# A fused adaLN attention block: projection steps get a pair of row maxima, and steps 105 to 120 do three maxima instead of four

## The chip, the cores and the metric

The kernel runs on one core of a Trainium2 chip. The metric is the device time of one execution in microseconds (us). A profiled execution gives, beside its time, a trace of every instruction on the engines: TensorE (PE, with its weight loads PEld), VectorE (DVE), ScalarE (ACT), GpSimd (POOL), SyncE (SP) and the DMA queues.

## The reference, cut to what matters

For one sequence of 2048 tokens with 448 features the block computes adaptive layer norm, 16-head attention with heads of 28 features, its output projection, a second adaptive layer norm and a GELU MLP.

```python
q, k, v = qkv[0], qkv[1], qkv[2]              # 16 heads of 28
scores = jnp.einsum("bhqd,bhkd->bhqk", q, k) * scale
p = _softmax(scores, axis=-1)                 # needs max over all 2048 keys of each row
o = jnp.einsum("bhqk,bhkd->bhqd", p, v)
x = x + ga * (o @ wo)                         # output projection, gated residual
h = _layernorm(x) * (1 + cb) + sb
x = x + gb * mlp(h)                           # LayerNorm, gelu(h @ w1 + b1) @ w2 + b2
```

## The kernel before

**Three stages.** A first stage builds q, k and v for all heads. The attention stage then runs 16 units of 16 steps, 256 steps in all. A unit is four heads (a group `g`, heads `j` = 0 to 3) and 512 queries (`qt`). Step `kt` of a unit takes 128 keys. The last stage is the MLP.

**One attention step.** PE forms the transposed scores of the four heads in two halves (L1305, 12 matmuls, 28 or 29 rows each). Each half fills a PSUM tile of two banks. ACT takes the exponential of each half into SBUF (L1318). PE then multiplies the exponentials *of the step before* with v into `o` (`av`, L1263). The 29th row of the scores carries minus the row maximum.

**Row maxima.** That maximum must be known before a unit starts, so the kernel computes scores of later units a second time with queries on partitions (`max_mm`, L476, one 28-row matmul of 512 keys) and reduces them on DVE over the free axis (L481). One unit needs 64 of these. They are spread over the steps of the units ahead of it. There are several ways to place them:

- `emit_single`: one matmul into one bank (`m1` or `m2`), one DVE reduction (L481).
- `open_pair` and `close_pair`: the difference of two key blocks (tile `d0h`) gives a matmul and a ReLU on ACT (L643). The step after next adds the second matmul and one DVE operation (L650), which together give two maxima.
- `emit_pair`: two matmuls of two heads next to each other into one PSUM tile of two banks, and one DVE reduction over both (L686). Where no two fitting maxima are left it falls back to two single ones in the same tile.

**Ring and no ring.** `RING` is the step from which a third two-bank tile `s2` is opened in place of the banks of `m2` (`third_tile`). From there a step does one `emit_single` into `m1` and one `emit_pair` into whichever of `s0` and `s2` the scores do not use. That is three maxima. `extra` can add a fourth when the maxima still to do, counted with the three per step to come, would miss a unit's start. Before `RING` a step does up to four singles (even steps) or three, or a closing and two singles (odd steps).

**Projection steps.** The last group's units project as they go. `is_wo` is true for steps 8 to 11 of units 12 to 15, which are steps 200 to 203, 216 to 219, 232 to 235 and 248 to 251. In each, after `av`, one token block is projected (`t_wo`, L396, a chain of 9 or 12 matmuls over 128 rows, called "the chain" below). ACT copies the result (L1052), POOL adds it to the residual. While maxima are left such a step is no ring step: `m2` takes the banks of `s2` back, scores go to `s1` and `s0`, and the step does `WO_MAX` = 3 singles. When no maxima are left, `three` becomes true and the scores rotate over `s1`, `s0` and `s2`.

The order of all instructions on each engine is the order in which this code is written out; no scheduler moves anything. A PSUM tile is written again only after its readers are done.

Of the kernel before, what the change touches and what calls it, by code (L numbers as in the profile page):

```python
# [31 lines left out]
NTT = S // 128  # L32
P1RATE = 4
LAST_MAX = NKT - 4
RING = 121
PAIR_AT = (2, 2, 0, 2)
PAIR_ROWS = {(0, 2): 2, (0, 3): 3, (1, 0): 2, (1, 1): 2, (1, 2): 3}
WO_MAX = 3
# [6 lines left out]
def tile_adaln_block(ctx: ExitStack, tc: tile.TileContext, x, wqkv, wo, w1, b1, w2, b2, c, w_mod, out):  # L45
# [29 lines left out]
    def nm(t):  # L75
        uid[0] += 1
        return f"{t}_{uid[0]}"
# [20 lines left out]
    def ps_two(key):  # L98
        return ps_pools[key][1].tile([128, 2, 512], F32, tag=key, name=nm(key), bufs=1)
# [403 lines left out]
    def load_hi(kind, g, b):  # L503
        loaded[(kind, g, b)] = clock[0] + (5 if clock[0] >= RING else 3)
        tg = ("kh" if kind else "qh") + str(b)
        t = sb.tile([128, 512], F32R, tag=tg, name=nm(tg), bufs=1)
        (kh_sb if kind else qh_sb)[(g, b)] = t
        sp.dma_start(f(t), f(dscr[kind][0][g])[:, b * 512 : (b + 1) * 512])
        if kind and b in (PAIR_AT[g], PAIR_AT[g] + 1) and all((g, PAIR_AT[g] + c) in kh_sb for c in range(2)):
            at(clock[0] + 4, lambda: make_kd(g))  # L510
# [81 lines left out]
    def there(kind, g, b):  # L592
        return (g, b) in (qh_sb, kh_sb)[kind] and loaded.get((kind, g, b), 0) <= clock[0]

    def ready_max():
        return [m for m in mxq if there(1, m[0], m[2]) and there(0, *m[:2])][: 24 if clock[0] >= RING else 64]

# [5 lines left out]
    def make_kd(g):  # L603
        if clock[0] >= RING:
            return
        if g and any(m[0] == kd["g"] for m in pairable()):
            at(clock[0] + 2, lambda: make_kd(g))
            return
        c0 = PAIR_AT[g]
        kd.update(g=g, t=slot("d0h", [128, 1, 512]), **{"from": clock[0] + 1})  # L610
        pool.tensor_tensor(out=kd["t"][:, 0, :], in0=f(kh_sb[(g, c0 + 1)]), in1=f(kh_sb[(g, c0)]), op=ALU.subtract)
# [4 lines left out]
    def pairable():  # L616
        return [
            m for m in mxq
            if m[2] == PAIR_AT[m[0]] and m[4] > 1 and other(m) in mxq and m[3] < PAIR_ROWS.get(m[:2], 4)
        ]  # L620

    def kept_back():
        kept = set()
        n = 0
        for m in pairable()[: (RING - clock[0]) // 2] if clock[0] < RING else ():
            n += 1
            if n <= (NKT * (m[0] * NB + m[1] - 1) + LAST_MAX - clock[0]) // 2 - 1:
                kept.update((m, other(m)))
        return kept
# [26 lines left out]
    def emit_single(half, ps):  # L656
# [9 lines left out]
        m = (alone or same[-2:] or fits or near)[0]  # L666
        if clock[0] < RING:
            kept = kept_back()
# [7 lines left out]
    def emit_pair(half, t):  # L676
        near = ready_max()
        for a, m in enumerate(near):
            n = m[:4] + (m[4] + 1,)
            if m[4] == 2 * half and n in near:  # L680
                mxq.remove(m)
                mxq.remove(n)
                g, qt, cch, i, j = m
                for jj in range(2):
                    max_mm(g, qt, i, j + jj, kh_sb[(g, cch)], lambda: t[:, jj])
                dve.tensor_reduce(out=mxp[(g, qt)][:, i, j : j + 2, cch], in_=t, op=ALU.max, axis=AX.X)  # L686
                count(g, qt, [cch, cch])
                return
        for jj in range(2):
            emit_single(half, lambda: t[:, jj])  # L690
# [38 lines left out]
    def finish_max(g, qt):  # L729
        if px_open and px_open[0][0][:2] == (g, qt):  # L730
            close_pair()
        while left[(g, qt)] > 0:
            emit_max(1)
# [47 lines left out]
    def load_q(u):  # L781
        g, qt = divmod(u, NB)
        qst[u] = load_parts(f"b{u % 2}", 0, g, slice(qt * 512, (qt + 1) * 512))
# [452 lines left out]
    three = False  # L1236


    def is_wo(s_):
        return s_ // NKT >= NU - NB and 8 <= s_ % NKT < 12  # L1240

    def extra(s_):
        if is_wo(s_):
            return False
        most = 0
        need = 0
        for v in range(s_ // NKT + 1, NU):
            need += left.get(divmod(v, NB), 64)
            rest = range(s_, NKT * (v - 1) + LAST_MAX)
            n_wo = sum(is_wo(x) for x in rest)  # L1250
            n_plain = len(rest) - n_wo
            if n_plain > 0:
                most = max(most, (need - 3 * n_plain - WO_MAX * n_wo) / n_plain)
        due[0] += min(most, 1)
        if due[0] < 1:
            return False
        due[0] -= 1
        return True

    def av(u, kt, p, o):  # L1260
        g = u // NB
        for j in range(4):
            pe.matmul(  # L1263
                o[32 * j : 32 * j + 32, :], v_sb[kt // 4][:, kt % 4, 4 * g + j, :], p[j // 2][:, j % 2, :],
                start=(kt == 0), stop=(kt == NKT - 1),
            )
# [4 lines left out]
    for u in range(NU):  # L1271
        g, qt = divmod(u, NB)
        for kt in range(NKT):
            step = u * NKT + kt
            if kt == 2 and u + 1 < NU and u + 1 not in qst:
                load_q(u + 1)
            clock[0] = step
            if kt == LAST_MAX and u + 1 < NU:
                finish_max(*divmod(u + 1, NB))
            tick_late()  # L1280
            if not (three or mxq or late):
                three = True
                s_ring[:] = ["s1", turns[step % 2], turns[1 - step % 2]]
            now[0] = turns[step % 2]
            was, ring = ring, step >= RING and (three or not is_wo(step))
            first = step % 2 if ring else 0
            pt = {hf: slot(tags[step % len(tags)], [128, 2, 512], F32) for hf, tags in zip((first, 1 - first), ptags)}
            if ring != was:
                third_tile(ring)
            more = ring and not three and extra(step)  # L1290
            late_one, after = after, more
            n_max = 0 if ring else WO_MAX if is_wo(step) else 4 - step % 2
            n0 = 1 if step % 4 == 3 and not is_wo(step) else 2
            closing = bool(px_open) and step % 2 == 1

            ks, qs = kst[(g, kt // 4)], qst[u]
            kc = slice((kt % 4) * 128, (kt % 4 + 1) * 128)
            for n, hf in enumerate((first, 1 - first)):
                s2 = ps_s2() if three else ps_two(now[0] if ring and n else ("s1", "s0")[n])
                for term, (kp, qp) in enumerate(((0, 0), (1, 0), (0, 1))):  # L1300
                    if ring and n == 1 and term == 2 and mxq:
                        emit_pair(first, ps_two(turns[1 - step % 2]))
                    for jj in range(2):
                        rows_ = slice(64 * hf + 32 * jj, 64 * hf + 32 * jj + DH + (term == 0))
                        pe.matmul(s2[:, jj, :], ks[rows_, kp, kc], qs[rows_, qp, :], start=(term == 0), stop=(term == 2))  # L1305
                    if closing:
                        if (n, term) == (0, 0):
                            close_pair()
                    elif n == 0 and term < n0 <= n_max:
                        emit_single(1, ps_mx)  # L1310
                    if n == 1 and term == 2:
                        for _ in range(2 if closing else n_max - n0):
                            emit_single(0, ps_mx)
                    if ring and (n, term) == ((1, 0) if late_one else (0, 0)) and not three:
                        emit_single(1 - first, ps_mx)
                    if n == 1 and term == 2 and more:
                        emit_single(first, ps_mx)
                act.activation(pt[hf], s2, AF.Exp, scale=SCALE)  # L1318
            if step == 0:
                v_task(NB - 1, 3, ps_mx())  # L1320
            if pend is not None:
                pu, pkt, pp, po = pend
                av(pu, pkt, pp, po)
                if pkt == NKT - 1:
                    end_unit(pu, po)
            if step % 2 and step + 2 < RING:
                open_pair()
            if kt == 0:
                o = ps_o()
            pend = (u, kt, pt, o)  # L1330
            if qt == NB - 1 and kt % 4 == 3 and g + 1 < NG:
                load_k(g + 1, kt // 4 if g else kt // 4 ^ 2)
            for fn in sched.pop(step, ()):
                fn()
# [115 lines left out]
```

## Time and profile before

| what | value |
|---|---|
| median of three runs | 1113.06 us (1112.14, 1113.06, 1167.62) |
| profiled execution, its time | 1112.02 us |
| span of its instructions | 1110.0 us |
| PE busy | 1098.9 us (99%) |
| DVE busy | 807.2 us (73%) |
| ACT busy | 693.0 us (62%) |
| POOL busy | 213.9 us (19%) |
| granted PE clock | 1.00 |

The span is the time from the first to the last instruction in the profile; the execution's own time is 2.0 us longer. Busy shares are means over three stages with different limits, so they say little of one step. One of the three runs is 5% above the other two.

### The profile page before, as it was taken

Reading aid. Unit: us, or ns where it says so; the run is one execution under the profiler, and the core shown is the slowest. Engines: PE = TensorE matmul, PEld = TensorE weight load, DVE = VectorE, ACT = ScalarE, POOL = GpSimd, SP = SyncE. Lnnn points to the kernel's source line nnn. Section 1 sums busy time; section 2 is a strip of 40 time slices with the busy share of each in tenths; the row PEclk is TensorE's granted clock in tenths of the full one; section 3 lists DMA queues with packets and bytes.
Section 4 is the critical chain, followed back from the end, with each engine's and each line's share of the span. In section 5 each row is a group of like instructions: output and inputs, shape, how many; then the busy total and the mean of one; then the engine's idle time right before and its main releaser. Section 6 shows DMA issues by size and latency. Waiting matters only on the chain.

```text
span 1110.0 us, 20703 instructions
## 1 busy us (share of the span) xinstructions
PE 1098.9 (99%) x8319; PEld 665.7 (60%) x8319; DVE 807.2 (73%) x1394; ACT 693.0 (62%) x877; POOL 213.9 (19%) x214
## 2 busy tenths in 40 slices
PE   8999999999999999999999999999999999999998
PEld 6756775444444444444444454545568888888887
DVE  6968788999999999988888867584558844434322
ACT  4565657888888888888888878677752311111210
POOL 1533333110000000000000020217215414023000
PEclk9999999999999999999999999999999999999999
DMA  9563263120231211221211402112222100000000
GB/s 309 204 195 102 88 204 112 51 68 30 79 94 42 81 34 52 73 83 48 88 31 59 130 24 88 58 30 78 72 82 67 32 34 1 2 32 1 34 1 34
DMA packets 49341, 81.19 MB, mean 73 GB/s; under 512 B 12311, under 2 KB 18702, under 8 KB 49234
## 3 DMA queue, kind: packets, MB, share of 16 engines
q1 hardware_dynamic: 48762, 79.14, 22.6%
q8 instruction: 65, 1.06, 0.4%
q10 hardware_dynamic: 148, 0.46, 0.1%
q0 software_dynamic: 336, 0.28, 0.1%
q14 instruction: 30, 0.25, 0.1%
HBM read 55.04 MB, written 26.48 MB: 73 GB/s over the span
## 4 chain that ended last, share of the span: by engine, by line
PE 95%; DVE 2%; ACT 1%; issue 1%; DMA 1%; SPq 0%; POOL 0%; DVEq 0%; ACTq 0%; POOLq 0%
PE s L1305 23%; PE o L1263 23%; PE m L396 16%; PE pa L396 9%; PE m L476 8%; PE s L1385 3%; PE s L1386 3%; PE s L1384 3%; PE s L476 2%; PE t L1385 1%; PE t L1386 1%; PE t L1384 1%; PE o L277 1%; DMA slot_c<-in_w_mod_dram 1%; DVE mxp L481 1%
## 5 line engine op out<-in xcount | busy, mean ns | idle before, releaser
L481 DVE TENSOR_REDUCE mxp<-m 128x1 f32<-128x512 f32 x563 | 364.6, 685 | 75.5 <-PE m L476 57.7
L1305 PE MATMUL s<-slot_b,slot_a 28*128 28x512 f32 (+1 forms) x3072 | 358.1, 424 | 0.3 <-ACT slot_c0h L1318 0.3
L1305 PEld LDWEIGHTS s<-slot_b,slot_a 28*128 28x128 f32 (+1 forms) x3072 | 210.9, 183 | 172.3 <-ACT slot_c L1318 93.9
L476 PE MATMUL m<-kh,qh 28*128 28x512 f32 x615 | 229.3, 468 | 0.6 <-DVE mxp L481 0.3
L1318 ACT ACTIVATE slot_c<-s 128x1024 f32<-128x1024 f32 x170 | 174.7, 1028 | 53.2 <-PE s L1305 52.3
L1263 PE MATMUL o<-slot_c,v 128*32 128x512 f32 x680 | 178.8, 605 | 0.0
L1361 ACT ACTIVATE full<-m,b_col 128x512 f32<-128x512 f32 x56 | 38.5, 688 | 191.9 <-PE m L396 179.7
L1263 PE MATMUL o<-slot_c1h,v 128*32 128x512 f32 x512 | 134.7, 605 | 0.9 <-ACT slot_c1h L1318 0.9
L1263 PE MATMUL o<-slot_c0h,v 128*32 128x512 f32 x512 | 134.7, 605 | 0.0
L1318 ACT ACTIVATE slot_c0h<-s 128x1024 f32<-128x1024 f32 x128 | 131.5, 1028 | 2.4 <-PE m L396 2.4
L1318 ACT ACTIVATE slot_c1h<-s 128x1024 f32<-128x1024 f32 x128 | 130.7, 1021 | 0.0
L686 DVE TENSOR_REDUCE mxp<-s 128x2 f32<-128x1024 f32 x103 | 126.2, 1226 | 5.1
L1364 DVE CAST hi<-full 128x512 fp32r<-128x512 f32 x56 | 25.5, 456 | 134.5 <-ACT full L1361 134.5
L1318 ACT ACTIVATE slot_d<-s 128x1024 f32<-128x1024 f32 x86 | 88.4, 1028 | 26.2 <-PE s L1305 25.5
L476 PEld LDWEIGHTS m<-kh,qh 28*128 28x128 f32 x615 | 92.0, 182 | 16.6 <-DVE mxp L481 13.1
L1019 POOL TENSOR_TENSOR osb<-osb,osb 128x512 f32<-128x512 f32 x16 | 21.0, 1314 | 363.6 <-DMA osb<-drec 220.9
L1263 PE MATMUL o<-slot_d,v 128*32 128x512 f32 x344 | 90.5, 605 | 0.4 <-ACT osb L1227 0.4
L396 PE MATMUL m<-y,slot_a 128*128 128x512 f32 x160 | 60.6, 395 | 0.0
L481 DVE TENSOR_REDUCE mxp<-ma 128x1 f32<-128x512 f32 x61 | 39.5, 681 | 13.3 <-PE m L476 8.9
L650 DVE CUSTOM_DVE_ANT_0 slot_d0i<-m,slot_d0i 128x512 f32<-128x512 f32 x54 | 37.3, 691 | 15.1 <-PE m L476 9.4
L1365 DVE TENSOR_TENSOR lo<-full,hi 128x512 fp32r<-128x512 f32 x56 | 43.8, 782 | 5.9 <-DVE hi L1364 0.9
L1263 PEld LDWEIGHTS o<-slot_c,v 128*32 128x32 f32 x680 | 24.5, 108 | 39.1 <-issue 36.6
(341 smaller groups left out, 1843.9 us busy)
## 6 DMA issues: line engine op xcount, KB each, us to landing
slot_b<-d SPq DMA_DIRECT2D x32, 256.0 KB
slot_a<-d SPq DMA_DIRECT2D x32, 256.0 KB
d<-lo SPq DMA_DIRECT2D x28, 256.0 KB
d<-hi SPq DMA_DIRECT2D x16, 256.0 KB
osb<-drec SPq DMA_DIRECT2D x15, 256.0 KB
out_dram<-xn SPq DMA_DIRECT2D x16, 224.0 KB
raw<-in_B_w_dram SPq DMA_DIRECT2D x14, 224.0 KB
qh<-d SPq DMA_DIRECT2D x12, 256.0 KB
```

What stands on the lines that cost most here:

```text
L396: pe.matmul(p, a, b, start=(i == 0), stop=(i == len(terms) - 1))
L476: pe.matmul(m, qh_sb[(g, qt)][js, i * 128 : (i + 1) * 128], k[js, :], start=True, stop=True)
L481: dve.tensor_reduce(out=mxp[(g, qt)][:, i, j, cch : cch + 1], in_=m, op=ALU.max, axis=AX.X)
L686: dve.tensor_reduce(out=mxp[(g, qt)][:, i, j : j + 2, cch], in_=t, op=ALU.max, axis=AX.X)
L1263: pe.matmul(o[32 * j : 32 * j + 32, :], v_sb[kt // 4][:, kt % 4, 4 * g + j, :], p[j // 2][:, j % 2, :], start=(kt == 0), stop=(kt == NKT - 1),
L1305: pe.matmul(s2[:, jj, :], ks[rows_, kp, kc], qs[rows_, qp, :], start=(term == 0), stop=(term == 2))
L1318: act.activation(pt[hf], s2, AF.Exp, scale=SCALE)
L1361: act.activation(gf, p, AF.Gelu_apprx_tanh, bias=b1_col[:, i : i + 1])
L1365: dve.tensor_tensor(out=glo, in0=gf, in1=f(ghi), op=ALU.subtract)
L1384: pe.matmul(pp, ghi[:, ts], w_hi, start=(m == 0), stop=False)
L1385: pe.matmul(pp, ghi[:, ts], w_lo, start=False, stop=False)
L1386: pe.matmul(pp, glo[:, ts], w_hi, start=False, stop=(m == NFT - 1))
```

## The change

`RING` goes from 121 to 105. In projection steps that still have maxima to do, a pair goes into tile `s1` after `av`, ahead of the chain. `extra` counts five maxima per projection step instead of three.

```diff
-RING = 121
+RING = 105
@@ extra
-                most = max(most, (need - 3 * n_plain - WO_MAX * n_wo) / n_plain)
+                most = max(most, (need - 3 * n_plain - (WO_MAX + 2) * n_wo) / n_plain)
@@ the attention loop
                 av(pu, pkt, pp, po)
+                if is_wo(step) and not three:
+                    emit_pair(step % 2, ps_two("s1"))
                 if pkt == NKT - 1:
                     end_unit(pu, po)
```

The total of maxima stays the same. Steps 105 to 120 did 64 of them and now do 48; steps 83 to 104 did 87 and now do 86. Steps 200 to 203 and 216 to 219 did 12 each and now do 20 each; steps 232 to 235 did 9 (three in each of 232, 233, 234) and now do 10 (five in 232 and 233). `extra` adds no fourth maximum in either kernel.

**Place 1, PE at step 105.** In these rows `s0`, `s1`, `s2`, `m1`, `m2` are PSUM tiles; L1305 are scores, L476 maxima, L1263 is `av`. Before:

```order
L1305 MATMUL s1_1472_5942<-slot_b0_1259_5100,slot_a2_976_3992 128x512 x2
L476 MATMUL m2_1473_5945<-kh0_1168_4740,qh1_970_3963 128x512
L1305 MATMUL s1_1472_5942<-slot_b0_1259_5100,slot_a2_976_3992 128x512 x4
L1305 MATMUL s0_1474_5953<-slot_b0_1259_5100,slot_a2_976_3992 128x512 x6
L476 MATMUL m1_1475_5960<-kh3_1234_4998,qh1_970_3963 128x512
L476 MATMUL m2_1476_5963<-kh3_1234_4998,qh1_970_3963 128x512
L1263 MATMUL o_1394_5642<-slot_c1_1462_5906,v2_231 32x512 x2
L1263 MATMUL o_1394_5642<-slot_c0h_1463_5907,v2_231 32x512 x2
L476 MATMUL m2_1477_5971<-slot_d0h_1269_5143,qh1_970_3963 128x512
```

And now:

```order
L1305 MATMUL s1_1468_5938<-slot_b0_1259_5100,slot_a2_976_3992 128x512 x2
L476 MATMUL m1_1469_5941<-kh2_1233_4996,qh1_970_3963 128x512
L1305 MATMUL s1_1468_5938<-slot_b0_1259_5100,slot_a2_976_3992 128x512 x4
L1305 MATMUL s2_1470_5949<-slot_b0_1259_5100,slot_a2_976_3992 128x512 x4
L476 MATMUL s0_1471_5954<-kh2_1233_4996,qh1_970_3963 128x512 x2
L1305 MATMUL s2_1470_5949<-slot_b0_1259_5100,slot_a2_976_3992 128x512 x2
L1263 MATMUL o_1392_5638<-slot_c1_1458_5898,v2_231 32x512 x2
L1263 MATMUL o_1392_5638<-slot_c0h_1459_5899,v2_231 32x512 x2
```

Two of the four maxima matmuls have become a pair in the free tile `s0`, the one with `d0h` is gone, and the second half of the scores is in `s2`.

**Place 2, PE at step 201, a projection step, from the second half of the scores to the start of the chain.** Here L396 is the chain. Before:

```order
L1305 MATMUL s0_2174_9075<-slot_b0_2005_8305,slot_a2_2071_8616 128x512 x6
L476 MATMUL m1_2175_9082<-kh3_1834_7509,qh2_1698_6888 128x512
L1263 MATMUL o_2109_8783<-slot_c1_2160_9011,v2_231 32x512 x2
L1263 MATMUL o_2109_8783<-slot_c0h_2161_9012,v2_231 32x512 x2
L396 MATMUL m2_2176_9090<-slot_e0_486_2027,slot_a2h_2087_8685 128x448
```

And now:

```order
L1305 MATMUL s0_2132_8981<-slot_b0_1963_8213,slot_a2_2029_8524 128x512 x6
L476 MATMUL m1_2133_8988<-kh2_1798_7456,qh2_1682_6917 128x512
L1263 MATMUL o_2066_8689<-slot_c1_2116_8910,v2_231 32x512 x2
L1263 MATMUL o_2066_8689<-slot_c0h_2117_8911,v2_231 32x512 x2
L476 MATMUL s1_2134_8996<-kh0_1717_7085,qh2_1682_6917 128x512 x2
L396 MATMUL m2_2135_9000<-slot_e0_486_2027,slot_a2h_2044_8591 128x448
```

Two maxima matmuls stand between `av` and the chain, in the tile that held the first half of this step's scores.

**Place 3, PE from the end of step 234's chain to the start of step 235's, where the maxima run out.** Before:

```order
L396 MATMUL m2_2434_10301<-slot_e0_486_2027,lo_2402_10153 128x448
L1305 MATMUL s1_2438_10319<-slot_b0_2238_9383,slot_a2_2071_8616 128x512 x6
L1305 MATMUL s0_2439_10327<-slot_b0_2238_9383,slot_a2_2071_8616 128x512 x6
L1263 MATMUL o_2352_9933<-slot_d0_2423_10260,v2_231 32x512 x2
L1263 MATMUL o_2352_9933<-slot_c0h_2424_10261,v2_231 32x512 x2
L396 MATMUL m2_2441_10343<-slot_e0_486_2027,slot_a2h_2330_9835 128x448
```

And now:

```order
L396 MATMUL m2_2400_10242<-slot_e0_486_2027,lo_2368_10093 128x448
L1305 MATMUL s1_2405_10270<-slot_b0_2200_9307,slot_a2_2029_8524 128x512 x6
L1305 MATMUL s2_2406_10278<-slot_b0_2200_9307,slot_a2_2029_8524 128x512 x6
L1263 MATMUL o_2318_9873<-slot_d0_2392_10212,v2_231 32x512 x2
L1263 MATMUL o_2318_9873<-slot_c0h_2393_10213,v2_231 32x512 x2
L396 MATMUL m1_2408_10294<-slot_e0_486_2027,slot_a2h_2296_9775 128x448
```

The maxima end one step sooner, so the third tile is opened one step sooner: step 235 writes its second half into `s2`, which takes the banks of the `m2` tile that step 234's chain has just filled.

## The prediction

> **What bounds the kernel now.** I read the chain that ended last first, to see which engine sets the end; then the windows view over three kinds of attention steps, to see what a step of each kind lasts; then the timeline of one projection step, to see where a pair would stand.
>
> ```profile
> PE 95%; DVE 2%; ACT 1%; issue 1%; DMA 1%; SPq 0%; POOL 0%; DVEq 0%; ACTq 0%; POOLq 0%
> 432.40:472.44 40.04, 40.04 (x387) 18.95 (x384) 36.46 (x69) 34.53 (x41) 2.67 (x4) 1.00 0.21 67
> 472.44:650.08 177.64, 177.64 (x1822) 76.61 (x1819) 154.46 (x182) 154.76 (x164) 13.33 (x15) 1.00 0.24 72
> ```
>
> 95% of the chain is PE, so time is won or lost where PE's order gets shorter or longer. In the windows view the first number after the stretch is its length, then come the busy times of PE, PEld, DVE, ACT and POOL. The first stretch goes from the first score matmul of step 105 to that of step 121, the second from there to step 200. How many steps lie in each is read from the score matmuls, 12 to a step, in the group view of the same two stretches:
>
> ```profile
> L1305 PE MATMUL s<-slot_b,slot_a 28*128 28x512 f32 (+1 forms) x192 | 24.4, 424 | 0.0
> L1305 PE MATMUL s<-slot_b,slot_a 28*128 28x512 f32 (+1 forms) x949 | 104.9, 424 | 0.0
> ```
>
> 192 / 12 = 16 steps of four maxima, 40.04 / 16 = 2.503 us each. 949 is 79 x 12 and one neighbour, so 79 ring steps of three maxima, 177.64 / 79 = 2.249 us each. In both, PE has no idle time, while DVE is busy 91% and 87% and ACT 86% and 87%. PE is the limit, with the other two close behind.
>
> Now one whole projection step, step 202, in the timeline (start, length, engine, line):
>
> ```profile
> 659.09 0.50 PE L1305 MATMUL s<-slot_b,slot_a 29*128 29x512 f32 x2
> 659.66 1.89 DVE L481 TENSOR_REDUCE mxp<-m 128x1 f32<-128x512 f32 x3 [2.28 <-PE m L476]
> 660.08 1.02 ACT L1318 ACTIVATE slot_c<-s 128x1024 f32<-128x1024 f32 x1 [0.36 <-PE s L1305]
> 660.24 0.62 PE L1263 MATMUL o<-slot_d,v 128*32 128x512 f32 x2
> 660.69 0.60 PE L1263 MATMUL o<-slot_d,v 128*32 128x512 f32 x2
> 661.24 0.88 PE L396 MATMUL m<-slot_e,slot_a2h 128*128 128x448 f32 x3
> 661.95 0.78 PE L396 MATMUL m<-slot_e,slot_a3h 128*128 128x448 f32 x3
> 662.57 0.57 PE L396 MATMUL m<-slot_e,hi 128*128 128x448 f32 x2
> 663.26 0.49 PE L1305 MATMUL s<-slot_b,slot_a 29*128 29x512 f32 x2
> ```
>
> The step lasts 663.26 - 659.09 = 4.17 us: scores with three singles 1.15, `av` 1.00, the chain 2.02. PE goes from one to the next without waiting for data. DVE waits 2.28 us before its three reductions and ACT is idle for more than half. So here a maximum's DVE and ACT work is free, and its PE time is not.
>
> **The change part by part.**
>
> *Ring from step 105.* It turns 16 steps at 2.503 us into ring steps at 2.249 us: 40.04 - 16 x 2.249 = **-4.06 us**. Steps 83 to 104 differ in one maximum of 87, and I cost that at nothing. The key blocks of the next groups are loaded up to four steps later than now, but their first use moves with them, never fewer steps behind the load than the least now, so no load becomes late.
>
> *A pair in ten projection steps (200 to 203, 216 to 219, 232, 233).* Its two matmuls use different 32-row groups. Where a maximum now shares PE with score matmuls it fills rows that these leave free; here nothing stands beside it. How much does a lone round of 28-row matmuls cost between two other kinds of matmul? The first stage has exactly that, four maxima of four row groups between two 128-row chains, and also a double round:
>
> ```profile
> 48.74 0.50 PE L476 MATMUL m<-raw,osb 28*128 28x512 f32 x1
> 49.18 1.20 PE L396 MATMUL pa<-slot_c,slot_a 128*128 128x512 f32 x4
> 106.79 0.50 PE L476 MATMUL m<-raw,qh 28*128 28x512 f32 x1
> 107.14 0.40 PE L476 MATMUL o<-kh,qh 28*128 28x512 f32 x1
> 107.46 0.74 PE L396 MATMUL pa<-slot_b,slot_a 128*128 128x512 f32 x2
> ```
>
> A lone round takes 49.18 - 48.74 = 0.44 us from its start to the next chain's start, two rounds 107.46 - 106.79 = 0.67. The pair is one round, as long as its two heads differ, which they do in all ten (in step 233 the pair falls back to two single maxima, of heads 0 and 1). So 10 x 0.44 = **+4.4 us**. Bounds: below, a matmul inside a chain costs (662.57 - 661.95) / 3 = 0.21 us, which a pair would cost if it joined its neighbours without a seam: +2.1. Above, two rounds: +6.7. I take 0.44, because the pair has another kind of matmul on both sides, as the lone round has.
>
> The Trainium skill ("TensorEngine Tiling (Array Packing)", Tiling Modes) says that a change of tiling mode drains TensorE, and the pair adds one such change per step; this speaks against the change, and the trace agrees: 0.44 us for a lone round against 0.23 for each further one (0.67 - 0.44). Without that rule the pairs would come to 10 x 0.23 = 2.3 us.
>
> The pair's DVE reduction is hidden. The pair of a ring step shows its price:
>
> ```profile
> L686 DVE TENSOR_REDUCE mxp<-s 128x2 f32<-128x1024 f32 x103 | 126.2, 1226 | 5.1
> ```
>
> In step 202 the three singles end on DVE at 659.66 + 1.89 = 661.55; the pair would start at 661.24 on PE, end about 0.50 later, and its reduction would end near 661.74 + 1.23 = 662.97. `s1` is written next by the following step's first scores, at 663.26 + 0.44 = 663.70: 0.7 us of cover. On the other side, the pair may write `s1` once this step's exponential of it is done, 660.08 + 1.02 = 661.10, and `av` keeps PE until 661.24: 0.14 us of cover. Both are enough, the second barely.
>
> *Step 234* loses its three singles; *step 235* opens the third tile a step sooner. Now they look like this:
>
> ```profile
> 751.53 0.50 PE L1305 MATMUL s<-slot_b,slot_a 29*128 29x512 f32 x2
> 756.31 0.99 PE L1305 MATMUL s<-slot_b,slot_a 29*128 29x512 f32 x12
> 756.48 0.53 ACT L1052 COPY full<-m 128x448 f32<-128x448 f32 x1 [1.77 <-PE m L396]
> 757.23 0.62 PE L1263 MATMUL o<-slot_d,v 128*32 128x512 f32 x2
> 760.88 0.51 PE L1305 MATMUL s<-slot_b,slot_a 29*128 29x512 f32 x4
> ```
>
> Step 234 (three singles) lasts 4.78 us, step 235 (none) 4.57: **-0.21 us**. In step 235 the second half of the scores will go to `s2`, on the banks where step 234's chain result lies until ACT has copied it, 756.48 + 0.53 = 757.01, 0.70 us into the step. Now both halves run side by side and `av` starts 757.23 - 756.31 = 0.92 into the step. With the second half held to 0.70 and three rounds long (0.67 + 0.23 = 0.90), `av` starts at about 1.60: **+0.7 us**. A bound from below is 0, if the copy's release is not waited for. From above, step 232, where PE waits in the same way for banks that change their owner, lasts 746.76 - 741.18 = 5.58 us against 4.78:
>
> ```profile
> 741.18 0.50 PE L1305 MATMUL s<-slot_b,slot_a 29*128 29x512 f32 x2
> 742.00 0.18 PEld L476 LDWEIGHTS m<-kh,qh 28*128 28x128 f32 x1 [0.52 <-ACT slot_c1h L1318]
> 746.76 0.50 PE L1305 MATMUL s<-slot_b,slot_a 29*128 29x512 f32 x2
> ```
>
> so 0.80 at most.
>
> *`extra`* changes no instruction, since it adds nothing in either kernel. ACT loses a few ReLUs and DVE a few reductions, where neither sets the end.
>
> Sum: -4.06 + 4.4 - 0.21 + 0.7 = **+0.8 us**. The span of 1110.0 would become 1110.8 and the profiled execution's 1112.02, with the same 2.0 around the span, 1112.8. The median shown, 1113.06, lies 1.04 above that execution and the lowest run, 1112.14, 0.12. I place the forecast between the two, **1113.3 us**: the gain at step 105 and the bill of the projection steps cancel.
>
> **The rivals.** Times are from the same base, 1113.3.
>
> *The pair costs no seam.* Had TensorE taken the pair along at 0.21 us and step 235 not waited, the sum loses 10 x 0.23 and 0.7: 1110.3 us, faster than before. For it: matmuls of one kind follow each other at 0.21, so PE can hide a weight load. Against it: the lone round of the first stage pays the seam on both sides.
>
> *The pair takes two rounds.* If its two heads did not overlap behind `av`, ten times 0.23 more: 1115.6 us. For it: two matmuls need two weight loads. Against it: four heads share one round in the first stage.
>
> *A hold on `s1`, slower.* The place is the first score matmul of the step behind each pair, which waits for DVE's reduction of `s1`. It decides once DVE has more than 0.7 us of other work between the third single and that write. If another piece as long as a pair's reduction stood there, each of ten steps would slip 1.23 - 0.7 = 0.5 us: 1118.3 us. For it: DVE also serves the second layer norm from step 231 on. Against it: that work is issued behind the pair in its step, and those steps are the long ones, with more cover.
>
> *The early ring steps gain nothing.* If steps 105 to 120 stayed at 2.503 us, because a late key load or ACT held them, 4.06 us are missing: 1117.4 us, slower. Against it: the 79 ring steps of now hold their mean across a change of group with all its loads.
>
> **How the numbers follow.** My forecast has a chance of 0.60, the seamless pair 0.15, two rounds 0.13, the hold on `s1` 0.07, no gain in the ring 0.05. The bounds of the terms give -4.06 + 2.1 - 0.21 + 0 = -2.2 and -4.06 + 6.7 - 0.21 + 0.8 = +3.2 us, so 1110.3 to 1115.7 on that base less the 0.8; the range takes in these and the spread of a run of about 1 us, and leaves out the last two rivals: **1110.2 to 1116.2 us**. A measurement of this kernel tells about 2% (22 us) from no change. No case here comes near that: within 2% 0.98, faster by more 0.005, slower by more 0.015, these two for what I have not seen.
>
> **What would show it.** Steps 105 to 120 should last 36.0 us instead of 40.04. A projection step with a pair should last 4.6 us (nine chain matmuls) or 5.2 (twelve), with the pair's first matmul where the chain's now starts and the chain 0.44 us behind it. DVE's pair reductions (L686) should go from 103 to 128. Step 234 should last 4.6 and step 235 5.3 us, with PE there waiting for the ACT copy of L1052. The forecast is wrong if steps 105 to 120 stay near 40 us, if a pair's step grows by less than 0.3 or more than 0.6 us, or if scores wait for a reduction of `s1`.

## The result and the profile after

The change makes the kernel a little slower: the median of 11 runs is 1115.28 us against 1112.07 us before, a ratio of 1.0028 with a 95% interval of 1.0019 to 1.0036. The profiled execution took 1115.36 us with a span of 1113.6 us, 3.6 more than the span before. The forecast was 1113.3 us in a range of 1110.2 to 1116.2, and within 2%; the time lies in the range, but the bill is larger than the sum of +0.8 us that stood behind it. One run of each kernel was far longer (2486.34 us of this one, 1167.62 of the one before), and the ratio leaves these two out.

The chain of waits still ends on PE, with the same shares as before, and the reductions over a pair rose from 103 to 128. These are the chain's row and the group of L686 in the page after:

```profile
PE 95%; DVE 2%; ACT 1%; issue 1%; DMA 1%; SPq 0%; POOL 0%; DVEq 0%; ACTq 0%; POOLq 0%
L686 DVE TENSOR_REDUCE mxp<-s 128x2 f32<-128x1024 f32 x128 | 156.9, 1226 | 8.9 <-PE s L476 2.9
```

The windows view after, cut at the first score matmul of steps 0, 105, 121, 200, 204, 216, 220, 232, 236 and 255, the last step of attention (the first number behind a stretch is its length, then come the busy times of PE, PEld, DVE, ACT and POOL); only the stretches that matter are shown, and the last one, from step 255 to the end, is called the tail:

```profile
166.98:432.92 265.94, 265.47 (x2519) 125.48 (x2518) 240.88 (x448) 225.96 (x263) 29.72 (x35) 1.00 0.22 65
432.92:468.93 36.01, 36.01 (x374) 15.62 (x370) 31.31 (x37) 30.96 (x34) 1.38 (x3) 1.00 0.23 71
646.55:665.64 19.09, 19.09 (x141) 11.28 (x137) 13.37 (x20) 10.01 (x12) 4.78 (x5) 1.00 0.01 3
692.49:714.19 21.70, 21.60 (x152) 13.56 (x148) 13.61 (x21) 10.15 (x12) 4.78 (x5) 1.00 0.03 7
741.09:763.58 22.49, 21.52 (x143) 13.16 (x139) 12.25 (x27) 10.10 (x12) 8.02 (x8) 1.00 0.03 7
814.68:1113.60 298.92, 292.23 (x1380) 249.85 (x1376) 142.80 (x262) 60.71 (x98) 62.24 (x51) 1.00 0.08 26
```

The three stretches of projection steps and the tail in the windows view before:

```profile
650.08:667.44 17.36, 17.36 (x134) 10.48 (x130) 8.27 (x14) 10.00 (x12) 4.73 (x4) 1.00 0.01 3
694.47:714.33 19.86, 19.86 (x145) 12.85 (x142) 8.46 (x16) 10.01 (x12) 4.77 (x5) 1.00 0.03 7
741.18:760.88 19.70, 19.61 (x141) 12.51 (x137) 10.61 (x25) 10.13 (x12) 8.21 (x8) 1.00 0.02 4
811.96:1110.00 298.04, 292.30 (x1380) 249.77 (x1376) 142.68 (x262) 60.78 (x98) 62.49 (x51) 1.00 0.08 26
```

So steps 105 to 120 give 40.04 - 36.01 = 4.03 us. Steps 200 to 203 take 19.09 - 17.36 = 1.73 us of it back, steps 216 to 219 take 1.84, steps 232 to 235 take 2.79. The tail is 0.88 longer, and the start, where nothing was changed, 166.98 instead of 166.44. Cut further, at each step's first score matmul, the steps last (us):

| step | before | after | difference | forecast |
|---|---|---|---|---|
| 200, 201, 202, 203 | 4.84, 4.17, 4.18, 4.17 | 5.28, 4.61, 4.58, 4.62 | 0.44, 0.44, 0.40, 0.45 | 0.44 each |
| 216, 217, 218, 219 | 5.46, 4.79, 4.81, 4.80 | 6.03, 5.20, 5.23, 5.24 | 0.57, 0.41, 0.42, 0.44 | 0.44 each |
| 232 | 5.58 | 5.99 | 0.41 | 0.44 |
| 233 | 4.76 | 6.67 | **1.91** | 0.44 |
| 234 | 4.79 | 4.55 | -0.24 | -0.21 |
| 235 | 4.57 | 5.29 | 0.72 | 0.7 |

One row of this table is off, step 233. Next to it an ordinary step with a pair, step 202, in the timeline after (start, length, engine, line):

```profile
656.44 0.50 PE L1305 MATMUL s<-slot_b,slot_a 29*128 29x512 f32 x2
658.57 0.50 PE L476 MATMUL s<-kh,qh 28*128 28x512 f32 x2
659.00 0.87 PE L396 MATMUL m<-slot_e,slot_a2h 128*128 128x448 f32 x3
659.11 1.23 DVE L686 TENSOR_REDUCE mxp<-s 128x2 f32<-128x1024 f32 x1 [0.24 <-PE s L476]
661.02 0.50 PE L1305 MATMUL s<-slot_b,slot_a 29*128 29x512 f32 x2
```

The pair's two matmuls start together, the chain follows 0.43 us behind, and the pair's reduction ends at 660.34, 0.68 before the next step begins. PE waits for nothing here. Step 233 in the timeline after:

```profile
747.08 0.50 PE L1305 MATMUL s<-slot_b,slot_a 29*128 29x512 f32 x2
749.40 0.50 PE L476 MATMUL s<-kh,qh 28*128 28x512 f32 x1
749.93 0.69 DVE L481 TENSOR_REDUCE mxp<-s 128x1 f32<-128x512 f32 x1 [0.42 <-PE s L476]
750.68 0.49 PE L476 MATMUL s<-kh,qh 28*128 28x512 f32 x1 [0.78 <-DVE mxp L481]
751.10 0.88 PE L396 MATMUL m<-slot_e,slot_a2h 128*128 128x448 f32 x3
753.75 0.98 PE L1305 MATMUL s<-slot_b,slot_a 29*128 29x512 f32 x12
```

Here the second matmul does not stand beside the first. It starts 1.28 us later, and the bracket says what it waited for: DVE's reduction of the first one. The fallback puts each of its singles in a bank of its own, but both write the tile `s1`, so the wait goes by the tile and not by the bank.

### The profile page after: what moved, and what is told of

Same layout as the page of the kernel before. It is cut to its first block, busy times and chain, and to the rows that moved or that the text cites. A ratio compares the mean times of both kernels' runs of the same rounds, so it can differ in the third digit from the quotient of the medians.

```text
span 1113.6 us, 20657 instructions
## 1 busy us (share of the span) xinstructions
PE 1100.5 (99%) x8319; PEld 664.9 (60%) x8319; DVE 813.3 (73%) x1369; ACT 688.8 (62%) x868; POOL 213.2 (19%) x214
## 4 chain that ended last, share of the span: by engine, by line
PE 95%; DVE 2%; ACT 1%; issue 1%; DMA 1%; SPq 0%; POOL 0%; DVEq 0%; ACTq 0%; POOLq 0%
PE s L1305 23%; PE o L1263 22%; PE m L396 16%; PE pa L396 9%; PE m L476 7%; PE s L1387 3%; PE s L1388 3%; PE s L1386 3%; PE s L476 2%; PE t L1387 1%; PE t L1388 1%; PE t L1386 1%; DMA slot_c<-in_w_mod_dram 1%; PE o L277 1%; DVE mxp L481 1%
## 5 line engine op out<-in xcount | busy, mean ns | idle before, releaser
L481 DVE TENSOR_REDUCE mxp<-m 128x1 f32<-128x512 f32 x529 | 343.9, 686 | 66.1 <-PE m L476 50.5
L1305 PE MATMUL s<-slot_b,slot_a 28*128 28x512 f32 (+1 forms) x3072 | 355.2, 424 | 0.3 <-ACT slot_c0h L1318 0.3
L1305 PEld LDWEIGHTS s<-slot_b,slot_a 28*128 28x128 f32 (+1 forms) x3072 | 209.9, 183 | 179.5 <-ACT slot_c L1318 98.9
L476 PE MATMUL m<-kh,qh 28*128 28x512 f32 x572 | 216.4, 469 | 0.7 <-DVE mxp L481 0.3
L1263 PE MATMUL o<-slot_c,v 128*32 128x512 f32 x680 | 178.9, 605 | 0.0
L686 DVE TENSOR_REDUCE mxp<-s 128x2 f32<-128x1024 f32 x128 | 156.9, 1226 | 8.9 <-PE s L476 2.9
L1263 PE MATMUL o<-slot_c1h,v 128*32 128x512 f32 x512 | 134.7, 605 | 0.9 <-ACT slot_c1h L1318 0.9
L1263 PE MATMUL o<-slot_c0h,v 128*32 128x512 f32 x512 | 134.7, 605 | 0.0
L1366 DVE CAST hi<-full 128x512 fp32r<-128x512 f32 x56 | 26.2, 468 | 135.7 <-ACT full L1363 135.7
L476 PEld LDWEIGHTS m<-kh,qh 28*128 28x128 f32 x572 | 86.1, 182 | 15.3 <-DVE mxp L481 11.4
L1263 PE MATMUL o<-slot_d,v 128*32 128x512 f32 x344 | 90.5, 605 | 0.4 <-ACT osb L1227 0.4
L396 PE MATMUL m<-y,slot_a 128*128 128x512 f32 x160 | 60.7, 395 | 0.0
L476 PE MATMUL s<-kh,qh 28*128 28x512 f32 x258 | 58.7, 446 | 0.9 <-DVE mxp L481 0.8
L1263 PEld LDWEIGHTS o<-slot_c,v 128*32 128x32 f32 x680 | 24.5, 108 | 37.5 <-issue 34.9
```

The costliest lines, as they stand in the source:

```text
L396: pe.matmul(p, a, b, start=(i == 0), stop=(i == len(terms) - 1))
L476: pe.matmul(m, qh_sb[(g, qt)][js, i * 128 : (i + 1) * 128], k[js, :], start=True, stop=True)
L481: dve.tensor_reduce(out=mxp[(g, qt)][:, i, j, cch : cch + 1], in_=m, op=ALU.max, axis=AX.X)
L1263: pe.matmul(o[32 * j : 32 * j + 32, :], v_sb[kt // 4][:, kt % 4, 4 * g + j, :], p[j // 2][:, j % 2, :], start=(kt == 0), stop=(kt == NKT - 1),
```

## The experiments

The theory after the first look: the early ring steps and nine pairs cost what was forecast; the surplus is the fallback of step 233. The rivals: the ring's gain is smaller and the pairs cheaper than they look, or the seam isn't a seam but the price of two heads. Ten kernels were run, and each ratio is against runs of the kernel before on the same chip. "Attention" is the time from step 0's first score matmul to that of step 255 in the profiled execution, 645.52 us before and 647.70 after.

**The early ring alone.**

```diff
 # from the kernel before
-RING = 121
+RING = 105
```

> RING is 105, no pair in the projection steps, and extra counts three maxima there as before the change. The planner then puts a fourth maximum into eleven ring steps between 113 and 200 and a few later ones, and the maxima run out in step 235. My theory, that the change is a sum of a ring gain and of pairs at 0.43 us: steps 105 to 120 take 36.0 us plus about 0.25 for one or two fourth maxima, against 40.04 before; projection steps 200 to 203 and 216 to 219 are as before (4.84, 4.17 to 4.18; 5.46, 4.79 to 4.81); a fourth maximum costs 0.25 us, the difference of a step of four and of three; in all 4.06 less, some 2.8 to 3.5 more, so 0.5 to 1.2 us faster than before. Rival, the early ring steps hurt something later (late keys, DVE phase): projection steps or the stage behind them grow without any pair, and the total is at least 1 us slower than before.

Measured: 1119.6 us against 1111.89, ratio 1.0071 (1.0059 to 1.0084), so a miss, and the slowest but one of all. Steps 105 to 120 last 36.84 us, still 3.2 shorter than before, and steps 200 to 203 last what they did before (4.85 in step 200, 4.16 in step 201). The loss is in the ring steps: steps 121 to 199 last 185.53 instead of 177.64, steps 204 to 215 28.19 instead of 27.03. Seventeen maxima that the changed kernel does in projection steps have to go elsewhere. Thirteen come back as fourth maxima of ring steps, one in step 113 and twelve between 121 and 215, because `extra` now finds them missing; two are done at one go ahead of step 220, where a unit's maxima have to be complete, and two in step 235. One of the fourth maxima, in step 137 of this kernel's timeline:

```profile
507.19 0.49 PE L476 MATMUL m<-kh,qh 28*128 28x512 f32 x1
507.61 0.62 PE L1263 MATMUL o<-slot_c,v 128*32 128x512 f32 x2
508.41 0.68 DVE L481 TENSOR_REDUCE mxp<-m 128x1 f32<-128x512 f32 x1
```

The matmul stands between scores and `av`, 0.42 us from its start to that of `av`, and its reduction is one more on a DVE that is 87% busy. From step 121 to the end of step 218 the kernel loses 8.72 us, so 8.72 / 12 = 0.73 us for each fourth maximum, against the 0.25 us that the theory had taken from steps of four and of three. Of this, 0.41 to 0.61 lie in the step itself and the rest in the steps behind it; how much of it is PE's and how much DVE's no run takes apart. The two ahead of step 220 make steps 219 and 220 longer by 1.83, since PE waits there for their reductions, once for 1.14 us. The early ring is worth its 4 us only because the pairs take its maxima.

**The pairs alone.**

```diff
 # from the changed kernel
-RING = 105
+RING = 121
```

> RING stays at 121, the pairs go into projection steps. Maxima then run out in ring step 229, so steps 232 to 235 have none and the third tile stays open through them. My theory: steps 105 to 120 take 40.0 us; the eight projection steps 200 to 203 and 216 to 219 grow by 0.41 to 0.44 us each (3.4 in all); steps 229 to 231 get shorter by 0.6 in all, step 232 loses its 0.8 us wait for banks that change owner, 233 and 234 lose 0.2 each; no step has the 1.9 us of step 233 in the changed kernel. Sum +1.5 us against before, within 0.7. Rival, a pair's cost shows only together with the early ring: projection steps as before, total below before.

Measured: 1113.93 us, ratio 1.002 (1.0011 to 1.0029); attention +1.74 us, as expected. Eight steps grow by 0.39 to 0.44 us; the maxima run out earlier, so that steps 232 to 235 last 4.73, 4.54, 4.56 and 4.54 us.

**A real pair in step 233.**

```diff
 # from the changed kernel
-    def emit_pair(half, t):
+    def emit_pair(half, t, either=False):
...
-            if m[4] == 2 * half and n in near:
+            if m[4] in ((0, 2) if either else (2 * half,)) and n in near:
...
-                    emit_pair(step % 2, ps_two("s1"))
+                    emit_pair(step % 2, ps_two("s1"), True)
```

A pair behind `av` has no score matmuls beside it, so it need not be of the heads that `step % 2` picks.

> The changed kernel, but the pair of a projection step may be heads 0 and 1 or heads 2 and 3, whichever is left, so step 233 finds a real pair (two matmuls, one reduction) instead of two single maxima that share tile s1. My theory: in step 233 the second single's matmul waits for the DVE reduction of the first, since both are in one tile; with a real pair step 233 falls from 6.67 to 5.2 us and the kernel is 1.4 to 1.5 us faster than the changed one. Rival, step 233 is long because DVE is late with the three singles and the second layer norm: step 233 stays above 5.8 us and the kernel gains less than 0.8.

Measured: 1113.25 us, ratio 1.0011 (1.0003 to 1.002). Step 233 in its timeline:

```profile
746.93 0.49 PE L1305 MATMUL s<-slot_b,slot_a 29*128 29x512 f32 x2
748.17 1.02 ACT L1318 ACTIVATE slot_c<-s 128x1024 f32<-128x1024 f32 x1 [0.60 <-PE s L1305]
749.25 0.18 PEld L476 LDWEIGHTS s<-kh,qh 28*128 28x128 f32 x2 [1.03 <-ACT slot_c L1318]
749.25 0.50 PE L476 MATMUL s<-kh,qh 28*128 28x512 f32 x2
749.68 0.87 PE L396 MATMUL m<-slot_e,slot_a2h 128*128 128x448 f32 x3
752.32 0.52 PE L1305 MATMUL s<-slot_b,slot_a 29*128 29x512 f32 x4
```

The two matmuls start together and the chain comes 0.43 us later: 752.32 - 746.93 = 5.39 us instead of 6.67, so 1.28 of the 1.47 us that step 233 cost beyond a pair. The wait of the fallback is shown. (Attention as a whole is 647.70 - 646.20 = 1.50 us shorter; the other 0.22 lie scattered over steps that the edit doesn't touch.) The last 0.19 have a cause of their own, in the rows of ACT and PEld: the exponential of `s1` ends at 748.17 + 1.02 = 749.19, and the pair may write `s1` only then. So it starts 2.32 us into the step, where the chain started at 2.14 before. The exponential, which waits for the scores of its half, starts 0.24 us later than before, and the second of the singles among the scores 0.57 us into the step instead of 0.02. By the code this single is of a head that shares its rows with these scores, since no others are left; no run tests that.

**The third tile not opened in projection steps.**

```diff
 # from the changed kernel
-            if not (three or mxq or late):
+            if not (three or mxq or late or is_wo(step)):
```

> The changed kernel, but the third tile s2 is never opened within projection steps, so step 235 keeps s0 for its second half. My theory, step 235 waits for the ACT copy out of the banks that s2 takes over: it falls from 5.29 to 4.57 us, nothing else moves before step 236, and the kernel is 0.7 us faster than the changed one. Rival, the 0.72 is DVE or POOL work of the second layer norm that is late behind the pair: step 235 stays at 5.3 us.

Measured: 1114.51 us, ratio 1.0023 (1.0014 to 1.0032). Step 235 in the timeline after, and then in this kernel's:

```profile
758.29 1.71 PE L1305 MATMUL s<-slot_b,slot_a 29*128 29x512 f32 x12
758.46 0.53 ACT L1052 COPY full<-m 128x448 f32<-128x448 f32 x1 [1.76 <-PE m L396]
759.04 0.53 PEld L1305 LDWEIGHTS s<-slot_b,slot_a 29*128 29x128 f32 x6 [0.22 <-ACT full L1052]
759.93 0.62 PE L1263 MATMUL o<-slot_d,v 128*32 128x512 f32 x2
763.58 0.52 PE L1305 MATMUL s<-slot_b,slot_a 29*128 29x512 f32 x4
```

```profile
757.32 0.98 PE L1305 MATMUL s<-slot_b,slot_a 29*128 29x512 f32 x12
758.23 0.62 PE L1263 MATMUL o<-slot_d,v 128*32 128x512 f32 x2
761.85 0.52 PE L1305 MATMUL s<-slot_b,slot_a 29*128 29x512 f32 x4
```

After the change `av` starts 759.93 - 758.29 = 1.64 us into the step, because half of the scores waits for the ACT copy (the PEld row, 0.75 us into the step); here it starts at 0.91, and the step lasts 4.53 us instead of 5.29. The term of +0.7 is shown, size and cause.

**One maximum behind `av` instead of two.**

```diff
 # from the changed kernel
-                most = max(most, (need - 3 * n_plain - (WO_MAX + 2) * n_wo) / n_plain)
+                most = max(most, (need - 3 * n_plain - (WO_MAX + 1) * n_wo) / n_plain)
...
-                    emit_pair(step % 2, ps_two("s1"))
+                    emit_single(step % 2, lambda t=ps_two("s1"): t[:, 0])
```

> The changed kernel with one single maximum (into one bank of s1) between av and the chain instead of a pair, so half the maxima matmuls and a DVE reduction of 0.69 instead of 1.23 us there; it does so in all twelve steps from 200 to 235 that project, since fewer maxima per step make the work last longer. My theory, the price of a pair is that of a lone round, one matmul length and a seam on both sides, whatever number of row groups it fills: each of these steps is 0.41 to 0.44 us longer than before the change, as with the pair. Rival, the two matmuls of the pair are paid one after the other, or DVE's longer reduction is: each grows by 0.2 to 0.25 us.

Measured: one run of 1114.38 us. Step 201 in its timeline:

```profile
654.37 0.50 PE L476 MATMUL s<-kh,qh 28*128 28x512 f32 x1
654.80 0.87 PE L396 MATMUL m<-slot_e,slot_a2h 128*128 128x448 f32 x3
656.82 0.49 PE L1305 MATMUL s<-slot_b,slot_a 29*128 29x512 f32 x2
```

One matmul holds the chain back by 654.80 - 654.37 = 0.43 us, as two did. Steps 201 to 203 last 4.59 to 4.60 us and 217 to 219 5.2, as with the pair. Step 200 is an exception with 4.87 us: the single behind `av` costs 0.42 there too, but the second single among the scores comes 0.31 us into the step instead of 0.70, so the wait for banks is that much shorter. Steps 234 and 235 are longer by 0.59 and 0.86, beyond the 0.41 to 0.44 expected: in both the exponential of `s1` ends 0.2 us late, as in step 233 above, and step 235 did no maxima before. Two of the maxima that are no longer taken show up as fourth maxima. So a pair costs what one maximum costs: the price is that of a round of its own, not of its heads.

**Both repairs**, that of step 233 and that of step 235 together (the two diffs above).

> The changed kernel with a real pair in step 233 (either half) and the third tile opened after the projection steps. My theory, the two repairs are independent: step 233 takes 5.2 to 5.4 us, step 235 4.5, steps 0 to 255 of the attention stage take 2.0 to 2.2 us less than in the changed kernel, which puts them level with before (within 0.3 us), and the kernel within 1.2 us of before. Rival, they share a cause (PE waiting for the same DVE or ACT work): together they bring no more than 1.5 us.

Measured: 1112.85 us against 1112.44, ratio 1.0003 (0.9994 to 1.0012). Attention is 645.56 us, level with 645.52 before. The forecast without its last term is +0.1 us. The terms come out at 4.01 less in steps 105 to 120, 4.66 more in the ten steps with pairs (0.63 of it in step 233) and 0.28 less in steps 234 and 235; the other steps are about 0.3 shorter, which nothing here explains.

**The ring kept in the projection steps**, on the kernel before, to see whether the wait for banks in steps 200, 216 and 232 can be avoided.

```diff
 # from the kernel before
-            was, ring = ring, step >= RING and (three or not is_wo(step))
+            was, ring = ring, step >= RING
...
-                    if ring and (n, term) == ((1, 0) if late_one else (0, 0)) and not three:
-                        emit_single(1 - first, ps_mx)
+                    place = (1, 1) if is_wo(step) or is_wo(step - 1) else (1, 0) if late_one else (0, 0)
+                    if ring and (n, term) == place and not three:
+                        emit_single(first if place == (1, 1) else 1 - first, ps_mx)
```

> The kernel before with one thing changed: from step 121 on the third tile stays open through the projection steps too, which then do as a ring step does (a pair in the free tile among the scores, one single in m1, here after ten score matmuls, since m1 holds the last chain until ACT has copied it). No pair after av. My theory, the first projection step of each unit pays 0.66 to 0.8 us for banks that change owner, and this falls away: steps 200, 216 and 232 come down to what 201, 217 and 233 take, the others stay within 0.2 us, 1.5 to 2.2 us faster than before. Rival, m1 alone is too little for a single and a chain: each projection step waits for DVE or ACT and grows by 0.3 us or more, so no gain.

Measured: 1121.76 us, ratio 1.0083 (1.007 to 1.0097), so the expectation fell. The wait for banks does go (step 200 4.38 instead of 4.84, step 216 4.99 instead of 5.46), but the other projection steps grow by 0.2 each, the ring steps behind them by 0.5 to 0.6 (steps 220 to 228, steps 204 to 215), and the end runs into the same fallback, in steps 230, 232 and 234. Of the 8.46 us that attention loses, 6.9 lie in steps 229 to 235. Step 234 of this kernel, 8.48 us long:

```profile
756.95 0.50 PE L476 MATMUL s<-kh,qh 28*128 28x512 f32 x1
758.09 0.68 DVE L481 TENSOR_REDUCE mxp<-s 128x1 f32<-128x512 f32 x1
758.82 0.49 PE L476 MATMUL s<-kh,qh 28*128 28x512 f32 x1 [1.38 <-DVE mxp L481]
```

Again two singles in one tile, 1.87 us apart instead of together; the pairs of steps 230 and 232 stand 1.19 and 1.77 us apart. What else makes these steps long no run takes apart.

**The ring kept, with pairs of either half and the early ring.** The edit of the ring just shown, on the changed kernel, with the real pair of step 233.

> The change with the ring kept through the projection steps: RING 105, a pair in the free tile among the scores, one single in m1, and a pair in s1 after av in steps 200 to 203, 216 to 219, 232 and 233. My theory by terms: 4.0 us less for the early ring, 10 pairs at 0.43 (4.3 more), 0.2 less for step 234, 1.5 to 2.2 less for the banks that no longer change owner, no 1.46 in step 233 and no 0.72 in step 235: 1.4 to 2.1 us faster than before. Rival, DVE becomes the limit of these steps with a single and two pairs: they grow by more than 0.6 us each and the kernel is no faster than before.

Measured: 1112.9 us against 1112.44, ratio 1.0008 (0.9999 to 1.0017): no gain. Step 200 lasts 4.81 us instead of 5.28, but steps 201 and 217 last 4.81 and 5.39 instead of 4.61 and 5.20. What the wait for banks returns, the single in its new place takes.

**A later second single in the first projection step of a unit.** In steps 200, 216 and 232 the second single needs `m2`, whose banks were those of `s2` and are read by ACT's last exponential of the step before. With `n0` = 1 it is issued behind all twelve score matmuls instead of behind the first four.

```diff
 # from the kernel before
-            n0 = 1 if step % 4 == 3 and not is_wo(step) else 2
+            n0 = 1 if (kt == 8 if is_wo(step) else step % 4 == 3) else 2
```

> The kernel before, but in the first projection step of units 12, 13 and 14 (steps 200, 216, 232) the second single is not issued among the first scores but with the third after them, when the exponential that still reads s2 is done and m2 may have its banks. My theory, the first projection step is 0.66 to 0.8 us longer than the others because PE waits at its second single for those banks: steps 200, 216 and 232 fall by 0.4 to 0.6 us each, the rest stays, 1.2 to 1.8 us faster than before. Rival, the wait only moves to the next instruction that needs m2, or scores and exponentials are what is late: less than 0.5 us in all.

Measured: 1111.68 us against 1112.65, ratio 0.9992 (0.9983 to 1.0001). Steps 200, 216 and 232 last 4.31, 4.89 and 4.93 us, 0.53, 0.57 and 0.65 less. Some of it is given back: steps 220 to 228 last 20.76 instead of 20.14, steps 233 and 234 0.2 more each. In attention 0.77 us are left. Step 200 in its timeline:

```profile
651.32 0.50 PE L1305 MATMUL s<-slot_b,slot_a 29*128 29x512 f32 x2
651.66 0.78 PE L1305 MATMUL s<-slot_b,slot_a 28*128 28x512 f32 x8
652.13 0.40 PE L476 MATMUL m<-kh,qh 28*128 28x512 f32 x2
652.61 0.62 PE L1263 MATMUL o<-slot_c1h,v 128*32 128x512 f32 x2
655.63 0.50 PE L1305 MATMUL s<-slot_b,slot_a 29*128 29x512 f32 x2
```

The scores run on without a stop, and `av` starts 1.29 us into the step.

**The change with both repairs and the later single.**

> The change with both repairs (a real pair in step 233, the third tile opened after the projection steps) and the second single late in steps 200, 216 and 232. My theory, the terms add: both repairs make it level with before, the late single takes 1.2 to 1.8 us off, so 1 to 1.8 us faster than before. Rival, the pair in these three steps waits for the later reductions or exponentials and the gain is under 0.5 us.

Measured: 1111.45 us against 1112.65 on the same chip, ratio 0.9988 (0.9979 to 0.9997). Attention is 643.48 us, 2.04 less than before the change. This is the only kernel here whose interval lies below 1; it beats both, by about 1.2 us the one before.

## Why the prediction was right, and where it failed

*The early ring steps, -4.06.* They gave 4.03 us. The rival that they gain nothing is out: 36.01 us for 16 steps leave no room for a late key load.

*The pair, 0.44 us.* Nine of ten cost 0.40 to 0.57, with a mean of 3.98 / 9 = 0.44. The price from the lone round of the first stage held in another stage, between other matmuls. Both pair rivals fall: a seamless pair would have cost 0.21, two rounds 0.67, and the kernel with one maximum shows 0.43 for one matmul as for two, so what is paid is the round by itself. The Trainium skill ("TensorEngine Tiling (Array Packing)", Tiling Modes: a change of mode drains TensorE) agrees with these 0.43 us; no run here takes the drain apart from the length of the round itself.

*Steps 234 and 235, -0.21 and +0.7.* They came out at -0.24 and +0.72, and the kernel that opens the third tile later gave 0.76 back, so the wait for the ACT copy is the cause.

*The step that failed: "which they do in all ten (in step 233 the pair falls back to two single maxima, of heads 0 and 1)".* The fallback was seen, and costed as one round, because its heads differ. That looked at PE's rows alone. The two singles share a tile that DVE must read between them, so they run one after the other with a reduction of 0.69 us in between: +1.91 us where 0.44 stood. A real pair in that step gave 1.28 us back. That the time lies in the range all the same is in part luck: the range reached up to 1116.2 for pairs of two rounds each, which did not come, and step 233 and the time outside attention filled the room left for them.

*The hold on `s1`.* It did not come: in step 202 the pair's reduction ends 0.68 us before the next step, as the 0.7 us of cover had said. The other cover, 0.14 us ahead of the pair, was enough in nine of the ten steps. In step 233 it was not: the exponential of `s1` ends 2.27 us into the step instead of 2.03 before, and the first matmul behind `av` starts at 2.32 instead of 2.14. These 0.18 us are what a real pair leaves of the surplus in step 233. Step 216 grew by 0.57, and the 0.13 beyond the others stand ahead of the pair, in the wait for banks, in the timeline after:

```profile
692.49 0.50 PE L1305 MATMUL s<-slot_b,slot_a 29*128 29x512 f32 x2
693.33 0.18 PEld L476 LDWEIGHTS m<-kh,qh 28*128 28x128 f32 x1 [0.54 <-ACT slot_c1h L1318]
```

and in the timeline before:

```profile
694.47 0.50 PE L1305 MATMUL s<-slot_b,slot_a 29*128 29x512 f32 x2
695.17 0.18 PEld L476 LDWEIGHTS m<-kh,qh 28*128 28x128 f32 x1 [0.40 <-ACT slot_c1h L1318]
```

The second single comes 0.84 us into the step instead of 0.70, behind ACT's last exponential of step 215.

*What was not in the sum at all.* The start and the tail, both of unchanged code, add 0.54 and 0.88 us to the profiled span. The start varies between 165.67 and 167.54 us over the kernels run, so it says nothing of the change. In the tail PE's last matmul starts 0.72 us later; what follows it lasts between 4.3 and 5.1 us over the kernels run, 0.2 more here than before. One row of the tail differs, the cast of L1364 (L1366 after). In the third stage before:

```profile
870.98 0.43 DVE L1364 CAST hi<-full 128x512 fp32r<-128x512 f32 x1 [0.95 <-ACT full L1361]
871.01 1.41 POOL L1095 TENSOR_TENSOR acc<-acc,row_b2g 128x448 f32<-128x448 f32 x1
```

And after:

```profile
873.76 1.43 DVE L1366 CAST hi<-full 128x512 fp32r<-128x512 f32 x1 [0.97 <-ACT full L1363]
873.76 1.15 POOL L1095 TENSOR_TENSOR acc<-acc,row_b2g 128x448 f32<-128x448 f32 x1
878.09 0.50 PE L396 MATMUL m<-y,slot_c1h 128*128 128x512 f32 x1 [0.88 <-DVE slot_c1h L1151]
```

Before, the cast starts 0.03 us ahead of the POOL operation and takes 0.43 us; after, both start at the same moment, the cast takes 1.43, and DVE is late enough that PE waits 0.88 us behind it. The wait is absent in eight of the ten other kernels, those with the early ring alone and with the pairs alone among them. In the two with the pair mended and with both repairs the cast takes 0.71 us and PE is 0.28 later from there on. Why the two engines meet differently there was not settled, nor whether the change is what moves them.

Added up over the profiled spans: -4.03 + 3.98 + 1.91 - 0.24 + 0.72 = 2.34 us, -0.17 in the other steps of attention, 0.54 at the start and 0.88 in the tail make 3.6. The forecast had +0.8 of it. The surplus in step 233 is 1.47, of which a run explains 1.28 and the rows of ACT the rest; the 1.4 at the start and in the tail is not forecast and only partly explained.

## What to carry to other kernels

A small matmul that runs beside others in one place costs a whole round where it stands alone, whether it is one row group or two, so work that fills gaps should be moved only to where a gap is, or be moved as the fullest round that fits. When a code path has a fallback, cost it by the tiles that it writes and who reads them in between, not by its engine's rows alone. A trade of two sums that nearly cancel, here 4.0 us against 4.4, is decided by its edge steps, the first, the last and the one where the work runs out, so cost these one by one.

## What was not expected of the hardware

A DVE cast of 128x512 took 0.43 us when it started 0.03 us ahead of a POOL operation and 1.43 us when both started at once, where it ended at 875.19, 0.28 us after the POOL operation's end at 874.91. In the first case the POOL operation took 1.41 us instead of 1.15. In the kernel with the pair mended a cast that starts while another POOL operation runs takes 0.71 us, and again ends 0.28 us after that operation's end. That is one operation held until the other is done rather than both slowed. The Trainium skill ("SBUF — State Buffer", Who interferes with whom) says that a cast in a two-port mode shares a port pair with GpSimd and that whichever of the two issues first holds it for its whole instruction. These cases agree with it; that this cast runs in a two-port mode no run here shows by itself. A fourth maximum in a ring step cost 0.73 us, three times what the steps of three and of four had suggested.
